# Splitting the first loads of a fused state-space and feed-forward kernel over two DMA queues

## The chip, the cores and the metric

The kernel runs on one core of a Trainium2 chip. A core has a matrix engine (TensorE, PE in the profile; its weight loads are shown as PEld), a vector engine (VectorE, DVE), an engine for activation functions (ScalarE, ACT), a general engine (GpSimd, POOL) and a synchronisation engine (SyncE, SP) that here does nothing but issue DMA transfers. An instruction that issues a transfer stands in the queue of its engine like any other; in the profile it appears as SPq (issued by SyncE) or ACTq (issued by ScalarE). The metric is the device time of one execution in microseconds. The kernel before takes 177.05 us, the median of three runs (176.91 to 177.43).

## What is computed

The input is normalised over its features, and two branches read the result: a diagonal state-space layer and a gated feed-forward layer. Their outputs are added to the input.

```python
x = A_x                                    # [1, 2048, 512] bf16
xn = layernorm(x)
# state-space branch: a complex first-order recurrence over 2048 steps, 512 states
dt = exp(log_dt);  Lam_bar = exp(dt * (Lambda_re + 1j * Lambda_im))
B_bar = ((Lam_bar - 1) / Lam)[:, None] * (B_re + 1j * B_im)
Bu = xn @ B_bar.T
h_t = Lam_bar * h_{t-1} + Bu_t
y_A = 2 * real(h @ C.T) + xn * Dskip
# feed-forward branch, F = 1376
y_B = (gelu(xn @ w_gate) * (xn @ w_up)) @ w_down
out = x + y_A + y_B
```

## The kernel before

The 2048 rows of x are worked in four blocks of 512, each of four tiles of 128 rows (tile 0 to tile 3 in block 0). A planner (class `Sched`) holds a list of operations with the buffers that they read and write. TensorE and SyncE keep the order in which operations are recorded; for ScalarE, VectorE and GpSimd the planner chooses the order from estimated durations. `order_behind` ties an operation behind another in its engine's order. Each transfer has a semaphore of its own, and whoever reads its buffer waits for it.

What matters here is the start, block 0, where nothing has been loaded yet. TensorE first runs matmuls on constants. Then it works through the first four feed-forward columns (the first 512 of 1376) before the layer norm of block 0 is known: each tile of x is centred on VectorE (`cent` for tiles 0 and 1, in two parts, with means from VectorE and ScalarE; `sub`, L951, for tiles 2 and 3, behind their statistics at L615 and L616), transposed by TensorE (`cent_T`, L684) and copied out of PSUM by ScalarE (L689). The products with the gate and up weights (`GT_k`, L701) then run in steps: k is the step along the 512 features, so step k needs rows 128k to 128k+127 of both weights. The steps of tiles 0 and 1 come first, in order of k; then tile 2 follows, and step 3. `GT_mm` (L712) computes the rest of tile 3 and the columns 512 to 895, for which a second pair of weight loads is needed.

The division by the standard deviation comes later. GpSimd takes the roots (L622), VectorE the reciprocals (L627) and the normalised tiles (L634). SyncE transposes these tiles by DMA (`TR`, L736) and so gives the operand of everything that follows: the rest of the feed-forward layer (`GU`, L843), and the state inputs (`BU`, L749), whose weights SyncE loads with transposing DMAs (`load_T`, L526). Between these, SyncE loads the x of blocks 1 and 2 (L482) and the skip vector (L535). `BU` of block 1 is halved: it starts with tiles 0 and 1 alone.

The transfers of the start are these. `ld_x0` (L497) loads one tile of x, 128 KB. `ld_wk` (L488) loads step k of one weight, 512 columns, 128 KB; `ld_w` (L493) loads all four steps of a group of columns: group 1 has 384 KB and group 2 has 480 KB. `load_par` (L510) loads three parameter rows of 1 KB each (log_dt, Lambda_re, Lambda_im); `tr_par` (L515) is a transposing DMA on SyncE that waits for all three and lays them across partitions.

In the kernel before, the built program has this order. SyncE: tile 0; gate and up of step 0, of step 1, of step 2; tile 3; gate and up of step 3; group 1 of both weights; group 2 of both; `tr_par`; the four tile transposes of block 0; x of block 1; the state weights; the skip vector; x of block 2; the tile transposes of block 1. ScalarE: a table load and a first activation, then tile 1; the three parameter rows; tile 2; then its first computing instruction, the mean of tile 1 (L956).

Of the kernel before, what the change touches and what calls it, by code (L numbers as in the profile page):

```python
# [365 lines left out]
def build(nc, ins, out):  # L366
    with ExitStack() as es:
        E = es.enter_context
        S = Sched(nc, es)
# [9 lines left out]
        WG = A.alloc("WG", [KD, F], BF16)  # L379
        WU = A.alloc("WU", [KD, F], BF16)  # L380
# [4 lines left out]
        WGc = [Buf("WGc%d" % i, "sbx", 10 * i, 10 * i + 1) for i in range(KD + 2)]  # L385
        WUc = [Buf("WUc%d" % i, "sbx", 100 + 10 * i, 101 + 10 * i) for i in range(KD + 2)]
# [34 lines left out]
        PROW = A.alloc("PROW", [128], BF16)  # L421
        PROW16 = Buf("PROW16", "sb", PROW.lo, PROW.hi, PROW.ap[0:16, :])
        PROWq = [Buf("PROW%d" % q, "prow", q, q + 1) for q in range(3)]
# [46 lines left out]
        GATE = {"before_gelu": [], "nh": 0}  # L470
        SCR = A.alloc("SCR", [1], F32)
        half = V(lambda e: e.memset(HALF.ap, 0.5), D_TINY, [], [HALF], "half")
# [10 lines left out]
                X_all.ap[:, 4 * b:4 * b + 4, :], x2[512 * b:512 * (b + 1), :].rearrange("(j p) d -> p j d", p=128)),  # L483
                512 * 1024, writes=X[4 * b:4 * b + 4], tag="ld_x%d" % b)

        def ld_wk(W, Wc, src, k):
            f0, f1 = FC[0]
            return S.dma(lambda e: e.dma_start(W.ap[:, k, f0:f1], src[128 * k:128 * (k + 1), f0:f1]),  # L488
                         256 * (f1 - f0), writes=[Wc[k]], tag="ld_w")

        def ld_w(W, Wc, src, n):
            f0, f1 = FC[n]
            return S.dma(lambda e: e.dma_start(W.ap[:, :, f0:f1], src[:, f0:f1].rearrange("(k p) f -> p k f", p=128)),  # L493
                         1024 * (f1 - f0), writes=[Wc[KD + n - 1]], tag="ld_w")

        def ld_x0(j, queue="sync", after=()):
            return S.dma(lambda e, j=j: e.dma_start(X[j].ap, x2[128 * j:128 * (j + 1), :]), 128 * 1024, writes=[X[j]], tag="ld_x0", queue=queue, after=after)  # L497
        ld_x0(0)
        GATE["par"] = S.order_behind(ld_x0(1, "scalar", [wrm]), GATE["table"])
        for k in range(KD):  # L500
            if k == 3:
                ld_x0(k)
            ld_wk(WG, WGc, ins["B_w_gate"], k)
            ld_wk(WU, WUc, ins["B_w_up"], k)
        ld_w(WG, WGc, ins["B_w_gate"], 1)
        ld_w(WU, WUc, ins["B_w_up"], 1)

        def load_par():
            for q, nm in enumerate(("A_log_dt", "A_Lambda_re", "A_Lambda_im")):
                GATE["par"] = S.order_behind(S.dma(lambda e, q=q, nm=nm: e.dma_start(PROW.ap[4 * q:4 * q + 4, :], ins[nm].rearrange("(s p) -> s p", p=128)),  # L510
                      1024, writes=[PROWq[q]], tag="ld_" + nm, queue="scalar", after=[half]), GATE["par"])
            GATE["par"] = S.order_behind(ld_x0(2, "scalar"), GATE["par"])

        def tr_par():
            S.dma(lambda e: e.dma_start_transpose(PAR.ap.rearrange("p q t -> p (q t)").unsqueeze(1), PROW16.ap), 4096,  # L515
# [434 lines left out]
        def sub(j):  # L950
            return V(lambda e: e.tensor_scalar(XN[j].ap, X[j].ap, MVt[0][j].ap[:, 0:1], None, ALU.subtract),  # L951
                     d_dve_ts4x(512), [X[j], MVt[0][j]], [XN[j]], "sub")
        load_par()
        load_W()
        tr_par()
# [103 lines left out]
def bass_parallel_sum__ssm_conv_s5__geglu_ffn__prompt_kernel(  # L1059
    nc: bass.Bass,  # L1060
    A_x: bass.AP,
    A_Lambda_re: bass.AP,
    A_Lambda_im: bass.AP,
    A_B_re: bass.AP,
    A_B_im: bass.AP,
    A_C_re: bass.AP,
    A_C_im: bass.AP,
    A_log_dt: bass.AP,
    A_Dskip: bass.AP,
    B_x: bass.AP,  # L1070
    B_w_gate: bass.AP,
    B_w_up: bass.AP,
    B_w_down: bass.AP,
    out: bass.AP,
):
    ins = {
        "A_x": A_x, "A_Lambda_re": A_Lambda_re, "A_Lambda_im": A_Lambda_im,
        "A_B_re": A_B_re, "A_B_im": A_B_im, "A_C_re": A_C_re, "A_C_im": A_C_im,
        "A_log_dt": A_log_dt, "A_Dskip": A_Dskip,
        "B_w_gate": B_w_gate, "B_w_up": B_w_up, "B_w_down": B_w_down,  # L1080
    }
    build(nc, ins, out)
# [28 lines left out]
```

## Time and profile before

| | |
|---|---|
| time, median of 3 runs | 177.05 us (176.91 to 177.43) |
| time of the profiled execution | 177.26 us |
| its span, first to last instruction | 175.9 us |
| TensorE busy | 172.8 us (98%) |
| VectorE busy | 159.7 us (91%) |
| ScalarE busy | 95.8 us (54%) |
| granted TensorE clock | 1.00 |
| DMA traffic | 14.36 MB, mean 82 GB/s |

The profile is one execution. Its span runs from the first to the last instruction; the 1.36 us between span and time lie around it. Busy is the time in which an engine works on an instruction; issuing a transfer isn't counted. Lines such as L701 are line numbers of the kernel before. In a timeline each row has a start, a length, the engine, the line, the operation and the tiles, and a bracket for the idle time just ahead of it with what ended it. The DMA rows give the time from the start of an issue to the landing of its last byte. In stages of the first 24.5 us the DMA engines were used like this:

| stretch, us | DMA share | GB/s | issuing queues |
|---|---|---|---|
| 2.0 to 3.0 | 0.97 | 329 | both, 128 KB loads |
| 3.0 to 4.4 | 0.73 | 193 | SyncE's loads, ScalarE's rows |
| 4.4 to 5.0 | 1.04 | 335 | both, 128 KB loads |
| 5.0 to 7.0 | 0.99 | 296 | SyncE's loads |

The DMA share is the mean busy share of the core's 16 DMA engines; it can come out over 1 where packets overlap.

### The profile page before, as it was taken

How to read it: one execution, taken by the hardware profiler on the slowest of the kernel's cores; microseconds unless marked ns; L12 is line 12 of the kernel's file. 1: busy time of each engine (PE TensorE's matmuls, PEld its weight loads, DVE VectorE, ACT ScalarE, POOL GpSimd, SP SyncE). 2: the span in 40 equal slices, each digit the busy share in tenths (PEclk: the TensorE clock that was granted, in tenths of full speed). 3: DMA queues.
4: the chain of work that ended last, by engine and by line, in shares of the span. 5: the costliest groups of instructions: out<-in, count | busy, mean ns of one | idle time of the engine just before them, and what ended most of it. 6: DMA issues, size and time to landing. Idle time of an engine off the chain costs nothing.

```text
span 175.9 us, 2549 instructions
## 1 busy us (share of the span) xinstructions
PE 172.8 (98%) x903; PEld 85.4 (49%) x903; DVE 159.7 (91%) x279; ACT 95.8 (54%) x187; POOL 10.7 (6%) x24
## 2 busy tenths in 40 slices
PE   7999999999999999999999999999999999999995
PEld 2645664744544444444644444444464444444454
DVE  6797999987999989889899999989999899999941
ACT  5367668999766899383676793000667970000000
POOL 3132120211000000002200000000000000000000
DMA  5999989975899000002015000002004000000311
GB/s 144 281 322 154 216 136 203 174 132 114 162 270 270 11 0 2 0 30 75 18 33 112 5 0 4 0 0 89 30 0 34 0 0 0 0 0 4 119 62 60
DMA packets 32421, 14.36 MB, mean 82 GB/s; under 512 B 23737, under 2 KB 32409, under 8 KB 32409
## 3 DMA queue, kind: packets, MB, share of 16 engines
q1 hardware_dynamic: 31952, 13.84, 36.9%
q10 hardware_dynamic: 456, 0.36, 0.6%
q8 instruction: 7, 0.11, 0.3%
q14 instruction: 6, 0.04, 0.1%
HBM read 6.46 MB, written 2.10 MB: 49 GB/s over the span
## 4 chain that ended last, share of the span: by engine, by line
PE 95%; DMA 2%; SPq 1%; issue 0%; DVE 0%
PE PS L885 37%; PE PS L843 32%; PE PS L749 16%; PE PS L712 4%; PE PS L817 3%; PE PS L701 2%; DMA arena<-in_B_w_up_dram 2%; SPq L488 1%; PE PS L684 0%; SPq L497 0%; DVE arena L903 0%
## 5 line engine op out<-in xcount | busy, mean ns | idle before, releaser
L885 PE MATMUL PS<-arena 128*128 128x512 bf16 (+3 forms) x323 | 66.2, 366 | 0.0
L843 PE MATMUL PS<-arena 128*128 128x512 bf16 (+1 forms) x272 | 58.1, 373 | 0.0
L885 PEld LDWEIGHTS PS<-arena 128*128 128x128 bf16 (+1 forms) x323 | 30.8, 98 | 35.2
L843 PEld LDWEIGHTS PS<-arena 128*128 128x128 bf16 x272 | 26.5, 98 | 29.5
L787 DVE TENSOR_TENSOR_SCAN arena<-arena 128x512 bf16<-128x512 f32 x32 | 38.9, 1256 | 0.0
L859 ACT ACTIVATE arena<-PS 128x512 bf16<-128x512 f32 x33 | 19.8, 599 | 26.2 <-DVE arena L903 16.7
L749 PE MATMUL PS<-arena 128*128 128x512 bf16 (+1 forms) x144 | 28.3, 355 | 0.1
L863 ACT ACTIVATE arena<-PS 128x512 bf16<-128x512 f32 x33 | 19.8, 599 | 5.4 <-PE PS L843 5.4
L749 PEld LDWEIGHTS PS<-arena 128*128 128x128 bf16 x144 | 14.0, 98 | 13.7 <-DMA arena<-arena 0.6
L877 ACT ACTIVATE PS<-arena 128x512 f32<-128x512 bf16 (+2 forms) x17 | 9.6, 582 | 19.7 <-DVE arena L903 19.0
L758 ACT ACTIVATE arena<-PS 128x512 bf16<-128x512 f32 x32 | 17.6, 597 | 1.6 <-PE PS L749 1.6
L903 DVE TENSOR_TENSOR arena<-PS,arena 128x512 bf16<-128x512 f32 (+2 forms) x17 | 10.9, 654 | 6.4 <-PE PS L885 6.4
L865 DVE TENSOR_TENSOR arena<-arena 128x512 bf16<-128x512 bf16 x33 | 13.2, 419 | 2.1 <-ACT arena L863 2.0
L776 DVE TENSOR_TENSOR arena<-arena 128x4096 bf16<-128x4096 bf16 (+1 forms) x5 | 9.2, 1859 | 0.4 <-ACT arena L611 0.4
L799 DVE TENSOR_TENSOR arena<-arena 128x4096 bf16<-128x4096 bf16 x4 | 9.2, 2291 | 0.1
L774 DVE TENSOR_TENSOR arena<-arena 128x4096 bf16<-128x4096 bf16 (+1 forms) x5 | 9.2, 1861 | 0.0
L800 DVE TENSOR_TENSOR arena<-arena 128x4096 bf16<-128x4096 bf16 x4 | 9.1, 2287 | 0.0
L615 DVE BATCH_NORM_STATS2 arena<-arena 128x6 f32<-128x512 bf16 x12 | 7.8, 685 | 0.9 <-DMA arena<-in_A_x_dram 0.7
L721 ACT ACTIVATE arena<-PS,arena 128x256 bf16<-128x256 f32 (+1 forms) x16 | 6.5, 450 | 3.3 <-DVE arena L621 1.5
L712 PE MATMUL PS<-arena 128*128 128x512 bf16 (+1 forms) x40 | 7.1, 336 | 0.0
L701 PE MATMUL PS<-arena 128*128 128x256 bf16 (+1 forms) x36 | 6.2, 308 | 0.2 <-DMA arena<-in_B_w_up_dram 0.2
L724 DVE SCALAR_TENSOR_TENSOR arena<-PS,arena 128x256 bf16<-128x256 f32 (+1 forms) x16 | 6.2, 444 | 0.0
(95 smaller groups left out, 124.2 us busy)
## 6 DMA issues: line engine op xcount, KB each, us to landing
out_dram<-arena SPq DMA_DIRECT2D x15, 128.0 KB, 1.7
arena<-in_A_x_dram SPq DMA_DIRECT2D x3, 512.0 KB, 6.3
arena<-in_B_w_down_dram SPq DMA_DIRECT2D x1, 1280.0 KB, 8.8
arena<-in_B_w_gate_dram SPq DMA_DIRECT2D x4, 128.0 KB, 3.4
arena<-in_B_w_up_dram SPq DMA_DIRECT2D x4, 128.0 KB, 3.6
arena<-in_B_w_gate_dram SPq DMA_DIRECT2D x1, 480.0 KB, 6.8
arena<-in_B_w_up_dram SPq DMA_DIRECT2D x1, 480.0 KB, 7.6
arena<-arena SPq DMA_TRANSPOSE x25, 3.3
```

The costliest lines, as they stand in the source:

```text
L701: PE(lambda e: e.matmul(dst, XCd(j, k), WGU[:, ws[0]:ws[-1] + 1, k, f0:f1], start=first, stop=k == KD - 1, skip_group_check=True), d_pe([w ...
L712: ins_ = e.matmul(dst, XCd(j, k), WGU[:, :, k, f0:f1], start=(k == 0), stop=(k == KD - 1))
L749: ins_ = e.matmul(PS[bank][:, 128 * j0:128 * j1], BBT[c][dk].ap[:, 128 * s:128 * (s + 1)], XNT[b].ap[:, dk, 128 * j0:128 * j1], start=(dk ...
L758: GATE["evBu"] = ACT(lambda e, bank=bank, k3=k3, s=s, c=c: e.activation(SSc[k3][s][c].ap, PS[bank][:, :], ACTF.Copy), d_act(512), [BANK[ba ...
L787: V(lambda e, g=g, rb=rb, init=init: e.tensor_tensor_scan(g.ap, rb, g.ap, init, ALU.mult, ALU.add), d_dve_scan(512), [g, PA[RRr]] + ([CARc ...
L843: ins_ = e.matmul(PS[bank][0:m, c0:c1], W.ap[:, dk, 128 * ft:128 * ft + m], XNT[b].ap[:, dk, c0:c1], start=(dk == 0), stop=(dk == KD - 1))
L859: GATE["last_gelu"] = ACT(lambda e, bg=bg, kk=kk, m=m: e.activation(GG[kk].ap[0:m, :], PS[bg][0:m, :], ACTF.Gelu_apprx_tanh), d_act(512), ...
L863: ACT(lambda e, bu=bu, kk=kk, m=m: e.activation(UPB[kk].ap[0:m, :], PS[bu][0:m, :], ACTF.Copy), d_act(512), [BANK[bu]], [UPB[kk]], "evU")
L865: V(lambda e, kk=kk, m=m, ft=ft, k2=k2: e.tensor_tensor(HTt[k2][ft].ap[0:m, :], GG[kk].ap[0:m, :], UPB[kk].ap[0:m, :], ALU.mult), d_dve_tt ...
L877: ACT(lambda e: e.activation(PS[bank][:, c0:c1], X[tt].ap[:, c0:c1], ACTF.Copy), d_act(c1 - c0), [X[tt]], [BANK[bank]], "seed")
L885: ins_ = e.matmul(PS[bank][:, c0:c1], l_[:, 128 * j:128 * (j + 1)], r_[:, c0:c1], start=False, stop=last and n == len(ops) - 1, skip_group ...
L903: V(lambda e: e.tensor_tensor(OUTB[ko].ap[:, c0:c1], PS[bank][:, c0:c1], XD[tt].ap[:, c0:c1], ALU.add), d_dve_1x(c1 - c0), [BANK[bank], XD ...
```

## The change

Seven transfers at the start change queue or place. ScalarE no longer issues the three parameter rows. After tile 1 it issues the up weights of step 0 and step 1, then tile 2, then the up weights of step 2. SyncE issues tile 0, the gate weights of steps 0, 1 and 2, tile 3, gate and up of step 3, then the three parameter rows, and then groups 1 and 2 of the weights as before. The parameter rows lose their explicit tie to a first VectorE instruction (`after=[half]`); they still wait for the GpSimd fill of their buffer. No computing instruction is added, removed or moved against the others on its engine.

```diff
-        def ld_wk(W, Wc, src, k):
+        def ld_wk(W, Wc, src, k, queue="sync"):
             f0, f1 = FC[0]
             return S.dma(lambda e: e.dma_start(W.ap[:, k, f0:f1], src[128 * k:128 * (k + 1), f0:f1]),
-                         256 * (f1 - f0), writes=[Wc[k]], tag="ld_w")
+                         256 * (f1 - f0), writes=[Wc[k]], tag="ld_w", queue=queue)
...
             ld_wk(WG, WGc, ins["B_w_gate"], k)
-            ld_wk(WU, WUc, ins["B_w_up"], k)
-        ld_w(WG, WGc, ins["B_w_gate"], 1)
-        ld_w(WU, WUc, ins["B_w_up"], 1)
+            if k < 3:
+                GATE["par"] = S.order_behind(ld_wk(WU, WUc, ins["B_w_up"], k, "scalar"), GATE["par"])
+            else:
+                ld_wk(WU, WUc, ins["B_w_up"], k)
+            if k == 1:
+                GATE["par"] = S.order_behind(ld_x0(2, "scalar"), GATE["par"])
 
         def load_par():
             for q, nm in enumerate(("A_log_dt", "A_Lambda_re", "A_Lambda_im")):
-                GATE["par"] = S.order_behind(S.dma(lambda e, q=q, nm=nm: e.dma_start(PROW.ap[4 * q:4 * q + 4, :], ins[nm].rearrange("(s p) -> s p", p=128)),
-                      1024, writes=[PROWq[q]], tag="ld_" + nm, queue="scalar", after=[half]), GATE["par"])
-            GATE["par"] = S.order_behind(ld_x0(2, "scalar"), GATE["par"])
+                S.dma(lambda e, q=q, nm=nm: e.dma_start(PROW.ap[4 * q:4 * q + 4, :], ins[nm].rearrange("(s p) -> s p", p=128)),
+                      1024, writes=[PROWq[q]], tag="ld_" + nm)
+            ld_w(WG, WGc, ins["B_w_gate"], 1)
+            ld_w(WU, WUc, ins["B_w_up"], 1)
```

## The prediction

> **What bounds the kernel now.** I read the chain of waits first, because TensorE is busy for 98% of the span and only what makes it late can change the end.
>
> ```profile
> 2.60 3.67 DMA arena<-in_B_w_up_dram
> 6.28 0.05 issue
> 6.32 1.26 PE PS L701 x10
> ...
> 24.61 6.91 PE PS L749 x32
> 31.52 0.12 issue
> 31.64 7.11 PE PS L749 x48
> ```
>
> Columns are start, length and what ran. TensorE is stopped twice by something outside itself. At 6.28 it gets the up weights of step 1 (issued at 2.60); its previous matmul began at 5.84 and these follow each other every 0.11 us, so it stood for 0.37 us. At 31.64 it begins the first half of block 1's state input (L749); the matmul before began at 31.14 and takes its 0.22, so 0.28 us are lost, 0.12 of it shown as "issue". From there to 174 no wait is left on TensorE: the table by stage gives 142.30 us busy in the 142.30 us from 31.7 to 174.0. So whatever the change does to the start counts only through the moment at which that L749 can begin.
>
> That L749 waits for transposed tiles 0 and 1 of block 1, and SyncE issues those. I therefore read SyncE's own timeline next.
>
> ```profile
> 7.82 1.99 SPq L515 DMA_TRANSPOSE arena<-arena  x1
> 10.27 5.15 SPq L736 DMA_TRANSPOSE arena<-arena  x4
> 15.46 0.58 SPq L482 DMA_DIRECT2D arena<-in_A_x_dram  x1
> 16.09 3.22 SPq L526 DMA_TRANSPOSE arena<-in_A_B_re_dram  x1
> 19.35 3.67 SPq L526 DMA_TRANSPOSE arena<-in_A_B_im_dram  x1
> 23.07 0.58 SPq L535 DMA_DIRECT2D arena<-in_A_Dskip_dram  x1
> 23.69 0.43 SPq L482 DMA_DIRECT2D arena<-in_A_x_dram  x1
> 24.17 2.40 SPq L736 DMA_TRANSPOSE arena<-arena  x1
> ```
>
> From 10.27 on every instruction begins 0.04 to 0.05 us after the one before it: one unbroken chain from block 0's first tile transpose to block 1's. Its only loose end is 9.81 to 10.27, where SyncE has finished the parameter transpose (L515) and waits for the first normalised tile. So I went to VectorE.
>
> ```profile
> 6.11 0.69 DVE L615 BATCH_NORM_STATS2 arena<-arena 128x6 f32<-128x512 bf16 x1 [0.74 <-DMA arena<-in_A_x_dram]
> ...
> 9.82 0.73 DVE L634 TENSOR_SCALAR arena<-arena 128x512 bf16<-128x512 bf16 x2
> ```
>
> VectorE stands 0.74 us for tile 2 of x and then works without a gap through three tiles' statistics to the normalisation at 9.82, 0.45 us ahead of SyncE's 10.27. So the moment that sets the whole kernel is tile 2's landing at 6.09: 6.09, to 9.82, to 10.27, to 24.17, to 31.64, to the end. Tile 2 comes from ScalarE's queue, issued at 2.66, and takes 3.4 us:
>
> ```profile
> arena<-in_A_x_dram ACTq DMA_DIRECT2D x1, 128.0 KB, 3.4
> ```
>
> **The change part by part.** The order of the compute instructions on all engines is the same in the two built programs; only the places of the DMA issues differ.
>
> *ScalarE.* Before: tile 1 at 1.00, three parameter rows (0.57, 0.27 and 0.31 us), tile 2 at 2.66, done at 3.02. After: tile 1, up 0, up 1, tile 2, up 2. ScalarE's own two 128 KB issues take 0.38 and 0.36 and follow 0.04 later, so up 0 is issued at 1.42, up 1 at 1.84, tile 2 at 2.26 and up 2 at 2.68, which ends at about 3.05. Tile 2's issue is 0.40 earlier. At SyncE's price (0.43 plus 0.05) it would be 2.38, 0.28 earlier, and the fifth issue would end at 3.3; behind it is the mean of tile 1 (L956, at 3.23), which would then be 0.1 late, and VectorE, with 0.74 idle, takes that up. So this queue costs nothing on the path.
>
> *Tile 2's flight.* Before, six 128 KB loads and three rows were issued ahead of it; after, seven loads (x0, gates 0 to 2, x1, up 0 and 1) and no rows. The trace has no such case, so I bound it. Upper end of the gain: the table by stage gives 329 GB/s from 2.0 to 3.0 and 335 from 4.4 to 5.0, where both queues carry 128 KB loads, but 193 from 3.0 to 4.4, at a DMA share of 0.73, where beside SyncE only the rows run. At some 332 GB/s the 270 KB of that stretch take 0.81 instead of 1.40 (0.59 saved), and the extra load costs 131 KB / 332 = 0.39. That lets tile 2 land 0.2 earlier than its issue alone gives: 0.60. VectorE can't use more than about 0.8, since its preceding work ends near 5.3. Lower end: the last eight of the twelve loads landed from 4.53 (up 0: issue 1.66 plus 2.9) to 8.77 (up 3: 4.98 plus 3.8), 0.53 us apiece though two queues were issuing. At that pace the eighth load lands five steps behind gate 0 (3.60), at 6.25: 0.16 late. I take the same flight of 3.4, since the one more load and the better filled stretch about cancel: landing at 5.69, **0.40 us earlier**.
>
> The Trainium skill ("DMA: Bandwidth & Descriptors", section "Issuing engines are not separate DMA queues") says that DMAs of all issuers run on the same 16 engines and that a second issuer saves only sequencer time, usually small beside the transfer. By that rule alone the gain is the issue's 0.40 at most and the transfer pace stays, which is the rival of the shared pace below; the 193 against 332 GB/s above speaks for idle engines in one stretch, so the trace agrees only in part.
>
> *Weights.* Up 0 is needed by TensorE at 4.86, gate 1 at 5.51, up 1 now at 5.95, gate 2 at 6.39, up 2 at 6.82. With up 1 issued at 1.84 instead of 2.60 and a flight of up to 3.8, it lands by 5.64, so the 0.37 us hole closes. That alone is worth nothing: TensorE would only wait longer at 31.64. From 7.0 on it is again tied to VectorE's centred tiles 2 and 3 (L951, 7.06 and 9.28), which move with tile 2, so it arrives at 31.64 early by the same 0.40.
>
> *SyncE.* Three weight loads and their 0.47 spacing go (1.42 us), three rows come, at ScalarE's prices 1.15 plus 0.13. The big loads (L493) are issued about 0.15 earlier, and so is the parameter transpose: 7.67, if its rows are there, ending at 9.66. The rows stand behind up 3 (issued at 3.56; by 3.4 to 3.8 us of flight it lands at 7.0 to 7.4) and are issued by about 4.95. I take them as landed by 7.7. The first tile transpose can then start at 9.87 (VectorE) against 9.70 (SyncE free): VectorE decides, with 0.17 to spare. The later loads (needed at 12.73, up weights landed at 11.95) keep their cover, because they too move earlier.
>
> *Beyond.* The state weights (L526) reach TensorE's 24.45 with 0.8 us to spare, and move with SyncE. TensorE's remaining waits past 31.64 had over 0.7 us of room, so a shift of 0.40 is carried to the end.
>
> *Sum.* Profiled execution: 177.26 for a span of 175.9, so 1.36 lie around the span, and this execution is 0.21 above the median of 177.05. Minus 0.40: span 175.5, time 176.86; against the median **176.65**. Its own range, with a gain of 0.2 to 0.6, is 176.45 to 176.85.
>
> **Rivals.**
>
> *Full rate on both queues.* If the loads run at 330 GB/s throughout, tile 2 lands 0.6 to 0.8 earlier. Then SyncE's parameter transpose becomes the bound: with the rows' issues at the cheapest (0.27 each) it starts at 7.35 and ends at 9.34, and the gain stops between 0.6 and 0.8: 176.25 to 176.45. For it: the 329 and 335 rows. Against it: 296 GB/s from 5 to 7 at a share of 0.99, so full engines don't always move 330.
>
> *Shared pace.* The 16 engines are the limit, tile 2 lands anywhere from 0.2 earlier to 0.16 later: 176.85 to 177.2. For it: the flight grows from 2.1 us (x0) to 3.8 (up 3) while issues continue, so a backlog exists. Against it: the 27% idle engines from 3.0 to 4.4.
>
> *The rows hold SyncE (slower).* The parameter rows now queue behind up 3, and L515, which needs them, stands ahead of the tile transposes on SyncE. If the twelve loads keep 0.53 apiece from 3.60, up 3 lands at 8.37 and the rows at 8.4 to 8.9; L515 then ends 2.04 later, at 10.45 to 10.95, and SyncE's chain starts 0.2 to 0.7 later: 177.25 to 177.75. It decides once the rows land after 8.2. For it: before, the rows were in by 7.8 without any wait, thanks to the other queue, and L515's 1.99 is paid in full after them. Against it: up 3 is issued 1.42 earlier, and it landed at 8.77 with 4.98.
>
> *It doesn't do what it says.* Excluded: the built order of both queues is as told.
>
> **How the numbers follow.** Measurement tells about 0.3% from no change, 0.53 us: below 176.52 is faster, above 177.58 slower. Chances: forecast 0.42, full rate 0.24, shared pace 0.17, rows 0.17. Faster: all of full rate and about 0.16 of the forecast's low half, 0.40. Slower: the rows' longer delays, and what I can't see, 0.15. The rest, 0.45, is within. The range takes in the full rate and the rows nearly whole: 176.2 to 177.7.
>
> **What would show it.** Right: tile 2's statistics on VectorE start near 5.7; no TensorE wait for up weights; L515 near 7.7; L736 near 9.87; the first half of L749 near 31.24, still after a short wait. Wrong: an L515 that starts after 8.2 and is followed at once by L736 (the rows); tile 2's statistics still near 6.1 (shared pace); or another wait on TensorE behind 31.6 that swallows the shift.

## The result and the profile after

The changed kernel takes 178.10 us, the median of 9 runs (177.46 to 178.45), against 177.14 (176.71 to 177.43, also 9) for the kernel before on the same chip: a ratio of 1.0053 with a 95% interval of 1.0036 to 1.0070. It is slower by about 0.96 us. The profiled execution took 178.41 with a span of 177.0, so it lies at the upper end of its runs, as the one of before (177.26) did of its own. Behind the edit all lines stand 4 further down: L619 is the L615 of before, L688 its L684, L740 its L736, L753 its L749.

The chain of waits of the kernel after, start, length and what ran:

```profile
1.41 0.45 ACTq L488
1.89 0.35 ACTq L488
...
2.37 5.14 DMA arena<-in_A_x_dram
...
7.54 0.70 DVE arena L619
...
8.27 0.19 DVE arena L620
...
8.48 0.36 DVE arena L955
...
8.89 0.40 PE PS L688 x4
9.29 1.89 PE PS L705 x9
...
26.04 13.85 PE PS L753 x80
```

The chain now goes through tile 2 itself. ScalarE issues it at 2.37, after two up weights, and it travels 5.14 us instead of 3.4. VectorE takes its statistics and centres it, and TensorE transposes it at 8.89 instead of 7.47. From there TensorE isn't stopped again: the 80 matmuls of L753 are one piece, where before they fell apart at 31.52. The last group of matmuls starts at 142.30; before it was 141.16. So the loss is 1.42 us at tile 2's transpose, less the 0.28 us of the wait at 31.6, which is gone: 1.14 us, and the span grew by 1.1.

VectorE's timeline of the kernel after (the bracket is the idle time ahead and what ended it) shows the same from the other side:

```profile
7.54 0.69 DVE L619 BATCH_NORM_STATS2 arena<-arena 128x6 f32<-128x512 bf16 x1 [2.00 <-DMA arena<-in_A_x_dram]
```

VectorE stands for 2.00 us, 1.26 more than before, for the tile that the change issues 0.29 earlier. SyncE's timeline of the kernel after:

```profile
4.02 0.37 SPq L513 DMA_DIRECT2D arena<-in_A_log_dt_dram  x1
...
8.36 1.23 SPq L519 DMA_TRANSPOSE arena<-arena  x1
11.69 5.15 SPq L740 DMA_TRANSPOSE arena<-arena  x4
...
17.52 3.77 SPq L530 DMA_TRANSPOSE arena<-in_A_B_re_dram  x1
21.33 2.59 SPq L530 DMA_TRANSPOSE arena<-in_A_B_im_dram  x1
...
25.26 5.27 SPq L740 DMA_TRANSPOSE arena<-arena  x4
```

The parameter transpose (L519) waits for its rows until 8.36 and ends at 9.59, 2.10 before the first tile transpose (L740), so SyncE waits there for VectorE and not for the rows. And although that tile transpose is 1.42 late, block 1's first one is only 1.09 late (25.26 against 24.17), and by the trace tile 1 of block 1 lands at 31.73 against 31.55.

Last, the table by stage of the kernel after. The columns that matter are the two at the right, DMA share and GB/s:

```profile
3.00:4.40 1.40, 1.40 (x8) 0.47 (x6) 0.98 (x5) 0.94 (x3) 0.00 (x0) 1.00 0.96 244
4.40:5.00 0.60, 0.50 (x4) 0.38 (x4) 0.60 (x3) 0.51 (x2) 0.00 (x0) 1.00 0.90 237
```

The slack stretch of before (193 GB/s at 0.73) is filled in share, but gives only 244, and the next one falls from 335 to 237. Over the whole of 1.5 to 6.0 us the table gives 260 GB/s after and 259 before; a second trace of the changed kernel gives 243. So filling the stretch brought no more bytes by 6.0.

### The profile page after: what moved, and what is told of

The parts are those of the page before. It is cut to its first block, busy times and chain, and to the rows that moved or that the text cites. A ratio compares the mean times of both kernels' runs of the same rounds, so it can differ in the third digit from the quotient of the medians.

```text
span 177.0 us, 2549 instructions
## 1 busy us (share of the span) xinstructions
PE 174.0 (98%) x903; PEld 86.3 (49%) x903; DVE 159.7 (90%) x279; ACT 95.4 (54%) x187; POOL 12.9 (7%) x24
## 4 chain that ended last, share of the span: by engine, by line
PE 94%; DMA 3%; DVE 1%; ACTq 0%; ACT 0%; issue 0%
PE PS L889 37%; PE PS L847 32%; PE PS L753 16%; PE PS L716 4%; PE PS L821 3%; DMA arena<-in_A_x_dram 3%; PE PS L705 2%; ACTq L488 0%; PE PS L688 0%; DVE arena L619 0%; ACT L474 0%; DVE arena L955 0%; DVE arena L907 0%; DVE arena L620 0%
## 5 line engine op out<-in xcount | busy, mean ns | idle before, releaser
L753 PE MATMUL PS<-arena 128*128 128x512 bf16 (+1 forms) x144 | 28.2, 355 | 0.0
L753 PEld LDWEIGHTS PS<-arena 128*128 128x128 bf16 x144 | 14.1, 98 | 13.3
L619 DVE BATCH_NORM_STATS2 arena<-arena 128x6 f32<-128x512 bf16 x12 | 7.8, 684 | 3.0 <-DMA arena<-in_A_x_dram 3.0
L705 PE MATMUL PS<-arena 128*128 128x256 bf16 (+1 forms) x36 | 6.9, 335 | 0.1
```

The lines of the kernel that those rows point to most:

```text
L705: PE(lambda e: e.matmul(dst, XCd(j, k), WGU[:, ws[0]:ws[-1] + 1, k, f0:f1], start=first, stop=k == KD - 1, skip_group_check=True), d_pe([w ...
L753: ins_ = e.matmul(PS[bank][:, 128 * j0:128 * j1], BBT[c][dk].ap[:, 128 * s:128 * (s + 1)], XNT[b].ap[:, dk, 128 * j0:128 * j1], start=(dk ...
```

## Experiments

In every one the two competing readings concern the loads of the first 9 us. The table collects what the traces gave. "Ahead" counts the 128 KB loads in front of tile 2 on its own queue. A load reports its completion in sixteen events in the trace, and its landing is the last of them; "transpose" is tile 2's first transpose on TensorE. Ratios are against the kernel before, from runs on the same chip. Each trace is one execution, so single landings can differ by some tenths.

| kernel | ahead | up 0 landed | tile 2 landed | transpose | median us | ratio (95%) |
|---|---|---|---|---|---|---|
| before | 1 | 4.53 | 6.09 | 7.47 | 177.14 | |
| after | 3 | 5.47 | 7.51 | 8.89 | 178.10 | 1.0053 (1.0036 to 1.0070) |
| after, again | 3 | 5.46 | 7.45 | 8.83 | 178.34, one run | |
| rows back on ScalarE | 3 | 5.07 | 6.79 | 9.89 | 179.54 | 1.0123 (1.0089 to 1.0157) |
| tile 2 first | 1 | 6.40 | 5.69 | 8.64 | 178.11 | 1.0061 (1.0041 to 1.0081) |
| SyncE held back | 3 | 5.43 | 6.70 | 8.08 | 178.82 | 1.0101 (1.0072 to 1.0130) |
| rows alone moved | 1 | 5.42 | 5.22 | 7.66 | 177.21 | 1.0012 (0.9998 to 1.0026) |
| tile 2 ahead of rows | 1 | 5.26 | 5.07 | 8.11 | 177.14 | 1.0007 (0.9996 to 1.0018) |
| one up weight | 2 | 5.07 | 5.97 | 7.44 | 177.87 | 1.0045 (1.0032 to 1.0057) |
| one up weight, rows on SyncE | 2 | 5.47 | 6.22 | 7.71 | 177.25 | 1.0018 (0.9996 to 1.0040) |
| tile 2 on SyncE | 5 | 4.75 | 5.98 | 7.85 | 177.03 | 1.0004 (0.9988 to 1.0020) |

The last event tells only part of it. Half of up 0 (eight of its sixteen events) had landed at 4.04 before, at 4.26 and 4.13 in the two traces of the changed kernel, and at 3.92 to 4.42 in the other kernels, except the one with tile 2 first (4.96). The last event came 0.49 behind the eighth before and 0.35 with tile 2 on SyncE, the two kernels in which ScalarE issues no 128 KB load right behind tile 1; in the other nine traces it came 0.82 to 1.51 behind. So what delays up 0 is its last parts. For tile 2 it is both: its eighth event is at 5.35 before and at 5.93 and 6.34 in the changed kernel, and its last one comes 0.74, 1.58 and 1.11 later. Why some parts fall behind when both queues have loads isn't shown.

**The changed kernel again**, unaltered.

> The changed kernel once more, for a second trace. Theory A (shared engines: the 16 DMA engines move the first loads at their own pace whichever queue issues them, so a load lands by how many 128 KB loads stand ahead of it or beside it; tile 2 has seven ahead and tile 3 beside it): tile 2's statistics on VectorE start at 7.0 to 7.6 again, most of the 16 parts of tile 2 landed by 6.7, span 176.3 to 177.3. Theory B (one stalled DMA engine in the profiled execution): tile 2's statistics start below 6.4 and the span is near 175.9.

178.34 us with a span of 177.0, tile 2's statistics at 7.47; fourteen of tile 2's sixteen events were in by 6.63 (expected: most by 6.7). The late tile is no accident of one execution.

**Rows back on ScalarE**, behind the last up weight; the rest of the change stays.

```diff
-                S.dma(lambda e, q=q, nm=nm: ...
-                      1024, writes=[PROWq[q]], tag="ld_" + nm)
+                GATE["par"] = S.order_behind(S.dma(lambda e, q=q, nm=nm: ...
+                      1024, writes=[PROWq[q]], tag="ld_" + nm, queue="scalar", after=[half]), GATE["par"])
```

> The changed kernel with the three parameter rows given back to ScalarE, behind the up weights of step 2; SyncE issues no rows. Theory A: the rows have no part in it; tile 2 still lands at 7.0 to 7.6, time 177.7 to 178.3. Theory C (the rows behind step 3 hold SyncE's parameter transpose and all behind it): the time falls to 177.0 to 177.4.

179.54 us, 1.2 above the top of the expected band. Tile 2 still lands late (6.79, though earlier than the expected 7.0 to 7.6), so the rows on SyncE aren't what makes it late. The miss in the time has a cause that shows in ScalarE's timeline of this kernel:

```profile
3.36 0.57 ACTq L513 DMA_DIRECT2D arena<-in_A_log_dt_dram  x1
3.96 0.27 ACTq L513 DMA_DIRECT2D arena<-in_A_Lambda_re_dram  x1
4.26 0.40 ACTq L513 DMA_DIRECT2D arena<-in_A_Lambda_im_dram  x1
4.71 0.63 ACT L960 ACTIVATE arena<-arena 128x512 bf16<-128x512 bf16 x1 [2.48 <-issue]
```

Eight issues stand ahead of ScalarE's mean of tile 1 (L960), which begins at 4.71 instead of 3.23; by the trace TensorE then stands 1.34 us for the last part of tile 1, until 5.85. The expectation had left out what the rows cost ScalarE's own computing with three weights ahead of them. That isn't the whole of it: behind this stop the 128x256 matmuls of this trace begin 0.21 us apart until 8.8 instead of 0.11 (last section), which I estimate at 1.4 us from the two spacings. Without it TensorE would have come to tile 2 no later than in the changed kernel. The six runs fall into two at 178.1 to 178.3 and four at 179.4 to 180.0; whether the slow spacing divides them isn't known.

**Tile 2 first**: ScalarE issues it right behind tile 1, then the three up weights.

```diff
         GATE["par"] = S.order_behind(ld_x0(1, "scalar", [wrm]), GATE["table"])
+        GATE["par"] = S.order_behind(ld_x0(2, "scalar"), GATE["par"])
...
-            if k == 1:
-                GATE["par"] = S.order_behind(ld_x0(2, "scalar"), GATE["par"])
```

> The changed kernel with tile 2 issued on ScalarE directly behind tile 1, ahead of the three up weights. Theory A: tile 2 lands by 5.3 and VectorE starts its statistics without a wait, but up 2 still lands near 8.2 and TensorE, which needs it ahead of tile 2's transpose, starts that transpose near 8.5 instead of 8.9: time 177.5 to 178.0. Theory D (tile 2 alone makes the loss): 176.5 to 177.1.

178.11 us, as slow as the change and 0.11 above the expected band. Tile 2 lands at 5.69 (expected by 5.3), and VectorE waits only 0.23 for it, but now up 0, and not up 2 as expected, is the late one. The chain of waits of this kernel:

```profile
1.89 4.51 DMA arena<-in_B_w_up_dram
...
6.45 2.36 PE PS L704 x20
8.80 0.22 PE PS L687 x4
```

TensorE stands 1.30 us for up 0 and reaches tile 2 at 8.64. The loss belongs to no particular load: in both kernels those that stand third and fourth on ScalarE's queue are late (up 0 and up 1 at 6.40 and 6.82 here, up 1 and tile 2 at 6.72 and 7.51 in the changed kernel).

**SyncE held back**: tile 3 and everything behind it on SyncE wait until tile 2 has landed, so that SyncE has only tile 0 and three gate weights in flight beside ScalarE's loads.

```diff
-                ld_x0(k)
+                GATE["x3"] = ld_x0(k)
...
-                GATE["par"] = S.order_behind(ld_x0(2, "scalar"), GATE["par"])
+                GATE["par"] = GATE["x2"] = S.order_behind(ld_x0(2, "scalar"), GATE["par"])
...
         S.schedule()
+        GATE["x3"].deps.append(GATE["x2"])
```

> The changed kernel in which SyncE waits for the landing of tile 2 ahead of its issue of tile 3, step 3 and all behind them, so that only gate 2 and up 2 run beside tile 2. Theory A: tile 2 lands at 5.6 to 6.3 and up 2 by 7.0, although both are issued at the same moments on the same queue as in the changed kernel; what is held back costs at most some tenths at step 3; time 176.9 to 177.6. A theory by which ScalarE's queue is slow in itself: tile 2 still lands past 7.0, time 177.9 or more.

Tile 2 lands at 6.70: 0.81 sooner than after, with the same queue and the same issue time, but not at the expected 5.6 to 6.3. Its eighth event comes 0.42 sooner than in the first trace of the changed kernel and 0.83 sooner than in the second. So the loads that SyncE issues from 2.60 on seem to take part in the delay, and those ahead of it account for the rest. How much each does isn't shown: with the rows back on ScalarE, where nothing is held back, tile 2 landed at 6.79, nearly as early. The time is worse still, 178.82, since what was held back is then late: the chain of waits of this kernel turns to the parameter transpose.

```profile
11.27 6.57 DMA arena<-arena
...
17.97 1.03 POOL arena L561
...
19.83 1.91 PE PS L847 x16
```

**Rows alone moved**: the kernel before, with only the three rows on SyncE behind step 3. Tile 2 is thereby issued at once behind tile 1.

```diff
-            for q, nm in enumerate(("A_log_dt", "A_Lambda_re", "A_Lambda_im")):
-                GATE["par"] = S.order_behind(S.dma(...queue="scalar", after=[half]), GATE["par"])
             GATE["par"] = S.order_behind(ld_x0(2, "scalar"), GATE["par"])
+            for q, nm in enumerate(("A_log_dt", "A_Lambda_re", "A_Lambda_im")):
+                S.dma(..., 1024, writes=[PROWq[q]], tag="ld_" + nm)
```

> The kernel before with one part of the change alone: the three parameter rows go to SyncE behind step 3, and so tile 2 follows tile 1 on ScalarE directly, issued near 1.4. All up weights stay on SyncE. Theory A, now with its second half (two queues with loads at once share the engines, so that each load ahead lands later, while the sum of bytes by 6 us stays at 8 to 9 loads): tile 2 lands at 4.6 to 5.3, VectorE has no wait for it; up 1, one load further back than before, lands at 6.3 to 6.8 and TensorE waits for it; tile 2's transpose starts at 7.4 to 7.9; time 176.7 to 177.4. Theory C (the rows on SyncE are what costs): 177.6 or more.

177.21 us, ratio 1.0012 (0.9998 to 1.0026): no measurable cost. Here the parameter transpose starts at 8.68, takes 1.28 and is followed by the tile transpose at 10.01, earlier than before (10.27). In this kernel up 0 is issued by SyncE at 1.66, to the hundredth as before, yet it lands at 5.42 instead of 4.53: the one thing new beside it is tile 2, issued on the other queue at about 1.4 instead of 2.66 (the rows, which stood there, are gone). Up 1 landed at 5.99, earlier than before and than the expected 6.3 to 6.8. The chain of waits of this kernel shows TensorE's stop for it:

```profile
1.66 3.76 DMA arena<-in_B_w_up_dram
5.42 0.05 issue
5.47 2.36 PE PS L701 x20
```

**Tile 2 ahead of the rows**, all still on ScalarE.

```diff
         def load_par():
+            GATE["par"] = S.order_behind(ld_x0(2, "scalar"), GATE["par"])
...
-            GATE["par"] = S.order_behind(ld_x0(2, "scalar"), GATE["par"])
```

> The kernel before with tile 2 ahead of the rows on ScalarE, all four still there. Theory A: as in rows_only for the loads (tile 2 at 4.6 to 5.3, up 1 at 6.3 to 6.8), time 176.7 to 177.4; the difference to rows_only is what the rows cost SyncE. Theory E (the place of the rows between tile 1 and tile 2 matters, because they slow the engines from 3.0 to 4.4): gate 1 and up 1 land 0.3 or more earlier than before, and the time falls below 176.7.

177.14 us, ratio 1.0007 (0.9996 to 1.0018). Tile 2 lands 1.02 earlier than before, up 0 lands 0.73 later, and the median stays. In this trace TensorE's early matmuls also ran at half pace (last section), so that it reached tile 2 only at 8.11; the median of 12 runs says that an early tile 2 alone buys nothing measurable. Up 1 landed at 5.80, again ahead of what was expected.

**One up weight** on ScalarE (up 0, then tile 2, then the rows), and **the same with the rows on SyncE** as in the change.

```diff
-            ld_wk(WU, WUc, ins["B_w_up"], k)
+            if k == 0:
+                GATE["par"] = S.order_behind(ld_wk(WU, WUc, ins["B_w_up"], k, "scalar"), GATE["par"])
+                GATE["par"] = S.order_behind(ld_x0(2, "scalar"), GATE["par"])
+            else:
+                ld_wk(WU, WUc, ins["B_w_up"], k)
```

> The kernel before with the up weights of step 0 alone given to ScalarE, between tile 1 and tile 2; the rows stay on ScalarE behind tile 2, so that ScalarE's mean of tile 1 waits for five issues and starts near 3.6 instead of 3.2. Theory A: tile 2 (five loads ahead) lands at 5.2 to 6.0, up 0 later than before (4.8 to 5.4); TensorE starts 0.3 to 0.5 later and then runs with less waiting; time 176.9 to 177.6. Theory F (issue time is the limit, each load taken off SyncE brings the rest forward): 176.2 to 176.7.

> As one_up, with the rows on SyncE behind step 3: ScalarE issues tile 1, up 0, tile 2 and no more. Theory A: tile 2 at 5.2 to 6.0, up 0 at 4.8 to 5.4, up 1 at 5.8 to 6.4; time 176.6 to 177.3, between the kernel before and the change (178.1) only if the share of loads on the second queue is what costs. Theory F: 176.0 to 176.6.

177.87 (1.0032 to 1.0057) and 177.25 (0.9996 to 1.0040). The first is 0.27 above its expected band, the second inside it. With one weight instead of three on ScalarE, tile 2 is third on its queue and lands at 5.97 and 6.22 (expected by 6.0). Yet the first keeps most of the loss, and only in the second, without the rows on ScalarE, is most of it gone. In the first the rows hold ScalarE's mean of tile 1 until 3.63, 0.40 later than before, and TensorE stands 0.32 for that tile. This may be what it loses, but the trace can't show it: the profiled execution of the first kernel (177.35) is the fastest of its 11 runs, and in it TensorE reaches tile 2 at 7.44, as before. These two kernels move 293 and 291 GB/s from 1.5 to 6.0 us, more than any other kernel here, and still gain nothing.

**Tile 2 on SyncE**: the kernel before, with tile 2 between up 1 and gate 2 on SyncE. After tile 1, only SyncE issues 128 KB loads.

```diff
             ld_wk(WU, WUc, ins["B_w_up"], k)
+            if k == 1:
+                ld_x0(2)
...
-            GATE["par"] = S.order_behind(ld_x0(2, "scalar"), GATE["par"])
```

> Kernel before, with tile 2 moved from ScalarE to SyncE, between up 1 and gate 2, so that after tile 1 only SyncE issues 128 KB loads, in order of need; ScalarE keeps the three rows. SyncE issues it at about 3.07, and everything behind it 0.47 us later than before. Theory (two queues make the loads share the engines and land later; one queue lets them land in its order): up 0, which landed at 4.53 in the kernel before and at 5.07 to 6.40 in every kernel that had a 128 KB load of ScalarE beside it before 2.7 us, lands at 4.4 to 4.7 again, up 1 by 6.3, and tile 2 at 6.4 to 6.9, a flight of 3.3 to 3.8 as the other loads of SyncE have. TensorE's first transpose of tile 2 is at 7.7 to 8.3; time 177.0 to 177.7. Rival (a single queue can't keep the engines busy, the second one is needed for the bandwidth): from 3.0 to 5.0 us the DMA moves less than 230 GB/s and tile 2 lands after 7.2; time 177.9 or more. If up 0 lands after 5.0 with no load beside it, the theory of sharing falls.

The loads land in SyncE's order: up 0 at 4.75, gate 1 at 5.12, up 1 at 5.42, tile 2 at 5.98, gate 2 at 7.09. Up 0 is 0.05 outside its band and tile 2 is earlier than expected. The rate over 3.0 to 5.0 is 228 GB/s, just inside what the rival named, but the landing that it tied to that rate (after 7.2) isn't there. The table by stage for 1.5 to 6.0 us, whose last two columns are DMA share and GB/s, of the kernel before:

```profile
1.50:6.00 4.50, 4.36 (x27) 2.15 (x25) 3.02 (x9) 2.87 (x8) 0.87 (x4) 1.00 0.85 259
```

of the kernel after:

```profile
1.50:6.00 4.50, 4.40 (x20) 2.07 (x19) 3.02 (x9) 2.71 (x8) 0.86 (x4) 1.00 0.90 260
```

and of this one:

```profile
1.50:6.00 4.50, 4.50 (x21) 2.21 (x20) 3.02 (x9) 2.87 (x8) 0.87 (x4) 1.00 0.85 235
```

One queue moved fewer bytes by 6.0 us (235 GB/s against 259 and 260; the second trace of the changed kernel has 243), and by then seven of the 128 KB loads had landed, tile 2 among them; in the kernels before and after it was five. Against the changed kernel every load from tile 1 to gate 3 lands earlier, though most of them are issued later: up 1 at 5.42 against 6.72, tile 2 at 5.98 against 7.51, gate 3 at 8.09 against 8.48. Only up 3, the last, is later (9.50 against 8.86).

This is the most direct evidence: with one queue tile 2 lands ahead of gate 2, in the order that the kernel needs, and its last event comes only 0.28 behind its eighth. Two queues don't always cost that: in the two kernels that give ScalarE an early tile 2 and no weights, seven loads had landed by 6.0 as well, only up 0 later.

The time is that of the kernel before, 177.03 us. No version tried is measurably faster than the kernel before.

## Why the prediction was wrong

It gave 176.65 us, a gain of 0.40, and the kernel lost about 0.96. The measured time lies above the upper end of the range, 177.7.

*The step that failed* is "Tile 2's flight", where I took "the same flight of 3.4, since the one more load and the better filled stretch about cancel". It measured 5.14. Two things were wrong in it. First, the price of filling the slack stretch: I let it run at 332 GB/s, and it gave 244, with the stretch behind it falling to 237. The total to 6.0 us didn't move. Second, and larger, I counted one more load ahead of tile 2, and by landings it was two more. In the kernel after the loads land in the order of issue, which goes back and forth between the queues: up 0 at 5.47 with gate 1 at 5.65, up 1 at 6.72 with gate 2 at 7.30, tile 2 at 7.51 with tile 3 at 8.01, up 2 at 8.23 with gate 3 at 8.48. Tile 2 is the eighth. Before, it stood second on ScalarE's queue, issued at 2.66, and landed sixth, at 6.09, ahead of up 1, which SyncE had issued a little earlier. ScalarE's short queue had been a way past SyncE's long one, and the change filled it with three weights, two of them ahead of tile 2. Besides, the last of tile 2's parts trailed further behind the rest than before (1.58 and 1.11 against 0.74), which no term of the sum had. Over all kernels, tile 2's flight is 3.4 to 4.3 when it is second on ScalarE's queue, 4.1 to 4.3 when it is third and 4.3 to 5.1 when it is fourth; as the later places are also issued later, it lands at 5.1 to 6.1, 6.0 to 6.2 and 6.7 to 7.5.

The Trainium skill states whose transfer goes next, in "DMA: Bandwidth & Descriptors", section "Queues, rings and completion order": each DMA engine takes turns between the queues that have work for it, packet by packet. The bytes of the two queues agree with it. From 3.0 to 6.0 us of the kernel after they are equal (packets, MB and share of the 16 engines; q1 is SyncE's queue, q10 ScalarE's):

```profile
q1 hardware_dynamic: 452, 0.41, 48.9%
q10 hardware_dynamic: 459, 0.42, 47.9%
```

From 4.5 to 5.0 us of the kernel before, ScalarE's queue, with tile 2 as its only 128 KB load, moved as much as SyncE's with several loads behind one another:

```profile
q10 hardware_dynamic: 97, 0.09, 54.0%
q1 hardware_dynamic: 90, 0.09, 49.1%
```

That explains how tile 2 overtook. It doesn't explain the late last parts of a load. I had weighed another section of that page, on what a second issuer saves, and not this one.

*ScalarE's issues.* Mis-sized a little: its two-weight pair took 0.93 and tile 2 and up 2 0.45 each, not 0.36 to 0.38, so tile 2 was issued at 2.37, the later of the two values given. The mean of tile 1 started at 3.40, 0.17 late, near the 0.1 named.

*Weights.* I expected the hole at up 1 to close. It moved: by the trace TensorE stands 0.14 at 5.52 for up 0 and 0.29 at 8.28 for up 2.

*SyncE and the carrying to the end.* Another step that failed is "one unbroken chain" from block 0's first tile transpose to block 1's, on which a shift would pass whole. It softened the loss. The chain looked rigid since each instruction began as the last one ended, but an issue's length isn't fixed work: the two state weights (L526 before, L530 after) took 6.89 before and 6.36 after, and block 1's first transpose moved by 1.09 for 1.42 at the start, the landing of tile 1 by 0.18. In block 0 the first transposed tile even landed earlier than before, 14.15 against 15.22, although its issue began 1.42 later. So the wait at 31.6 vanished, and the end was set by TensorE alone, through tile 2's transpose at L688. Nor did an early tile 2 alone move the end: in the kernel with tile 2 ahead of the rows it landed 1.02 us sooner and block 1's tile 1 0.99 sooner (30.56), but TensorE came to tile 2's transpose 0.64 later than before and ran on from there without a stop.

*Rivals.* "Full rate on both queues" fell with the 244 GB/s of the stretch at a share of 0.96. "Shared pace" was right that no more bytes move, and had the wrong size; its bound of 6.25 for tile 2 took 0.53 us a load from before's landings, and the five landings of after from gate 0 (3.71) to tile 2 (7.51) took 0.76 apiece. By the eighth events they took 0.48, and 0.57 in the second trace, so the pace it assumed held for the middle of the loads and missed the late last parts. "The rows hold SyncE" had the right sign for a wrong reason: the rows landed by 8.26 and L519 began at 8.36, past the 8.2 that I named, but its issue took 1.23 and not 1.99, and VectorE was later anyway. Moving the rows alone cost nothing measurable.

## What to carry to other kernels

In this kernel a second queue for the first loads wasn't a second lane of bandwidth. Ask which load is next on each queue: a load that was needed early and was alone on a short queue overtook the others, and it lost that when more loads were put ahead of it. Where loads are needed in a known order and the engines are near full, try one queue in that order first; here it landed the first weights and tile 2 sooner than two full queues, though the time only came back to that of before. Look at a load's last event and not at its rate, since its reader waits for the last part. And the length of an issue isn't fixed, even in a chain that looks back-to-back, so don't carry a shift along such a chain without a check of how its lengths vary.

## What the runs showed of the hardware that I had not expected

*Early matmuls at half pace under a granted clock of 1.00.* Two matmuls with 256 columns, then three transposes, in TensorE's timeline of the kernel before:

```profile
4.47 0.38 PE L701 MATMUL PS<-arena 128*128 128x256 bf16 x2
4.69 0.33 PE L684 MATMUL PS<-arena 128*128 128x128 bf16 x3
```

and of the kernel with tile 2 on SyncE:

```profile
4.55 0.61 PE L702 MATMUL PS<-arena 128*128 128x256 bf16 x2
4.96 0.53 PE L685 MATMUL PS<-arena 128*128 128x128 bf16 x3
```

In the second the 128x256 matmuls begin 0.21 us apart instead of 0.11, although both profiles show a clock of 1.00. Most of what this kernel could have gained seems to have gone there. TensorE in it never waits from 0.77 to the end, while before it lost 0.65 us in two waits; but it reached tile 2's transpose at 7.85 against 7.47, so that L750 began 0.27 later than L749 before and only used up the wait at 31.6. The slow stretch was there in the profile of after (to 6.7 us) and not in its repeat, with a span of 177.0 in both, so it isn't what made the change slower. It differs between executions of one kernel. The Trainium skill ("TensorE: Matmul & The Clock Gate", section "Part 1: The HAM clock gate") tells of a half-rate start whose length varies from run to run. The spacings agree, and the granted clock in the profile doesn't show it. What decided it in each execution was not tried.

*The length of an issue.* The parameter transpose, the same instruction, took 1.99 us of SyncE's time before, 1.23 after, 1.28 with the rows alone moved, 2.37 with tile 2 on SyncE and 2.50 with tile 2 ahead of the rows. Over all eleven traces those issued from 7.18 to 8.15 took 1.99 to 2.50, those from 8.20 on 1.18 to 1.34. That they wait for room behind earlier transfers would fit, but no run separates it.
